# Two matmul passes for three in the values of a batch's last 64 tokens

## The chip, the cores and the metric

The kernel runs on one core of a Trainium2 chip. The metric is the device time of one execution in microseconds (us), and of several runs the median. Engines are named as in the profile: PE is TensorE's matmul, PEld its weight load, DVE is VectorE, ACT ScalarE, POOL GpSimd, SP SyncE, which here issues the DMAs.

## The reference, cut to what matters

Three layers follow each other on 8 batches of 576 tokens with 512 features: an attention over 32 memory slots, a token and channel mixing layer, and a last layer with four attention experts of head size 64. The change lies in the last layer:

```python
def _moe2_ref(x, w_gate, wq, wk, wv, wo):
    logits = x @ w_gate                    # 4 experts, the best 2 of a token count
    ...
    for e in range(E):                     # E = 4, Hd = 64
        q, k, v = x @ wq[e], x @ wk[e], x @ wv[e]
        scores = scale * (q @ k.transpose(0, 2, 1))
        ...                                # causal mask, softmax
        ye = a @ v @ wo[e]
        ...                                # ye is weighted by the gate of its token
```

The inputs are float32 and so is the result. A float32 matrix product is made here from three products of rounded parts: a matrix X is kept as a high part Xh (X rounded to the type fp32r that TensorE takes) and a low part Xl = X - Xh, and X W is taken as Xh Wh + Xh Wl + Xl Wh.

## The kernel before, in words

The kernel has three stages, one for each layer, in one program. In the last stage, which fills the time from about 694 us to the end, a batch's 576 tokens are five chunks of rows: four of 128 tokens and one of 64 (`rows`, `NQ = 5`, `ST = 64`, `SM = 512`). Tokens lie along the free axis of `xh[b]` and `xl[b]` (128 partitions x `KD = 4` pieces of the 512 features x 576 tokens).

`mm2_2(j, c)` makes piece c of half-batch j of this x (j = 2b and 2b + 1): a matmul into the PSUM ring `g`, an addition on DVE, the high part on ACT, the low part on POOL (L1233 to L1235). `load_2`, `load_p2`, `split_2` and `mm1_2` prepare the same layer of mixing for later half-batches; so the end of the second layer runs inside the last stage.

`values(b, c)` makes values and gate logits of chunk c: the chunk's tokens are the stationary operand (up to 128 columns), and the moving operand is `vgh` or `vgl`, high and low part of the 260 columns of `wv` (4 x 64) and `w_gate` (4). `mm3` (L250) issues 12 matmuls for it, three for each of the four feature pieces; with `late="l"` the four that use the low part of x come last. Then ACT copies the values' high part to the tiles `vhl` and `vh3` (shown as `vh`, L1280) and the logits to `lg` (L1281, for the last chunk once more into the lower half, L1283), and DVE writes the low part beside it (L1285). For the chunk of 64 tokens ACT copies the finished 64 rows to partitions 64 to 127 as well (L1287), since the weights of its tokens are used there for a second expert.

`gates(b, ...)` turns the logits of all five chunks into the gate (DVE, one exponential on ACT; L1297 to L1320), `norm(n)` multiplies the softmax of expert n with it (L1369 to L1371 on DVE, L1379 on POOL), `turn` and `tail_turn` transpose the result on PE (L1398 to L1418), and `weigh` multiplies by the values (L1443), adds the two halves of the PSUM tile through the scratch tile `yb` (a copy on ACT, L1445, an addition on DVE, L1446), and splits the sum (L1449, L1450 on POOL; L1461 and L1462 for the tokens of the last chunk). `project` multiplies by `wo` and sends the output. For the last batch the tiles of `project` are in a pool `late`, which takes memory that other tiles have left; the projections of three earlier batches (`HELD`) are kept for the last batch as work between (`fetch`, L1469, loads them again).

PSUM is shared out in rings: `g` has 3 buffers (`GB`), `s` and `t` have 2, `y` has 1. The order of the instructions in this stage isn't the order of the code: the program is built with a planner that simulates the engines with costs of its own and puts an instruction into its engine's queue when its operands would be there. So a matmul of one product may stand between those of another, as the rows below show. The order is fixed once the program is built; on the chip each engine's queue runs strictly in it. SP's queue is one too, with all DMA issues of this stage: loads (L875, L879), the swaps between `qa` and `qb` (L1264, L1265), the queries of the last tokens to `qz` (L1345), and outputs (L1498 to L1501).

Of the kernel before, what the change touches and what calls it, by code (L numbers as in the profile page):

```python
# [10 lines left out]
F32 = mybir.dt.float32  # L11
F32R = mybir.dt.float32r
BF16 = mybir.dt.bfloat16
I32 = mybir.dt.int32
U32 = mybir.dt.uint32
AF = mybir.ActivationFunctionType
# [11 lines left out]
def f(ap):  # L28
    return ap.bitcast(F32)
# [181 lines left out]
def fused_kernel(ctx: ExitStack, tc, q, k, v, phi, w_tok1, w_tok2, w_ch1, w_ch2,  # L211
                 w_gate, wq, wk, wv, wo, out):
    nc = tc.nc
    B, H, S, D = q.shape
# [4 lines left out]
    E = wq.shape[0]  # L219
    KD = DM // 128  # L220
# [3 lines left out]
    SM = 512  # L224
    ST = S - SM
    scale = 1.0 / float(D) ** 0.5

    PE, ACT, DVE, POOL, SP = nc.tensor, nc.scalar, nc.vector, nc.gpsimd, nc.sync
# [5 lines left out]
    consts = ctx.enter_context(tc.tile_pool(name="consts", bufs=1, reuse_waits="tile"))  # L234
    ident = consts.tile([128, 128], F32, name="ident")
    make_identity(nc, ident[:])
    consts.tile([128, 8], F32, name="edge")
    still = consts.tile([128, 128], BF16, name="still")
    DVE.memset(still[:], 0.0)

    def mm3(ps, pairs, start=True, stop=True, late=None):

# [74 lines left out]
    with ExitStack() as sa:  # L317
# [9 lines left out]
        t1l = wa.tile([128, 5, T], F32R, name="t1l")  # L327
        t2h = wa.tile([128, 2, S], F32R, name="t2h")
        t2l = wa.tile([128, 2, S], F32R, name="t2l")
        ones = wa.tile([128, 16], F32, name="ones")  # L330
        DVE.memset(ones[:], 1.0)
        vmask = wa.tile([128, 4, 64], F32, name="vmask")
# [569 lines left out]
    with ExitStack() as sb:  # L902
# [194 lines left out]
        for i in range(NW + LAG):  # L1097
            items = [()] if i == NW else [work[i]] if work[i][0] in WIDE else [(*work[i], 0), (*work[i], 1)]
            for it in items:
# [63 lines left out]
                if it and n == NBLK - 1 and fcs == [0]:  # L1163
                    sw_ctx.close()
                    wkx_ctx.close()
                    stg = stg_ctx.enter_context(tc.tile_pool(name="stgc", bufs=2, reuse_waits="tile"))
                    wcp = ctx.enter_context(tc.tile_pool(name="wcp", bufs=1, side="right"))
                    qkh = wcp.tile([128, 2, KD, E * 64], F32R, name="qkh")
                    qkl = wcp.tile([128, 2, KD, E * 64], F32R, name="qkl")
                    vgh = wcp.tile([128, KD, E * 64 + 16], F32R, name="vgh")[:, :, 0:E * 64 + E]  # L1170
                    vgl = wcp.tile([128, KD, E * 64 + 16], F32R, name="vgl")[:, :, 0:E * 64 + E]
                    woh = wcp.tile([128, 2, DM], F32R, name="woh")
                    wol = wcp.tile([128, 2, DM], F32R, name="wol")
                    w3 = w3_ctx.enter_context(tc.tile_pool(name="w3", bufs=1, side="right"))
                    wcl = chload()
# [10 lines left out]
    with ExitStack() as sc:  # L1186
# [10 lines left out]
        POOL.tensor_copy(tmask[ST:128, :], cmask[ST:128, SH + ST:S + ST])  # L1197
        qz = wk_.tile([128, 2, 2, 128], F32R, name="qz")
        POOL.memset(f(qz[:]), 0.0)
        tri = wk_.tile([128, E, E], F32, name="tri")  # L1200
        POOL.memset(tri[:], 1.0)
        POOL.affine_select(out=tri[:], in_=tri[:], compare_op=OP.is_gt, fill=0.0, base=0,
# [2 lines left out]
        NQ = 5  # L1205
# [17 lines left out]
        def mm2_2(j, c):  # L1223
            b = j // 2
            if j % 2 == 0 and c == 0:
                xh[b] = wk_.tile([128, KD, S], F32R, name="xh", bufs=1)
                xl[b] = wk_.tile([128, KD, S], F32R, name="xl", bufs=1)
            p = pp.tile([128, 512], F32, name="g", bufs=GB)[:, 0:SH]
            mm3(p, [((w2h[fc][:, c, :], w2l[fc][:, c, :]), (h2[j, fc][0][:], h2[j, fc][1][:]))
                    for fc in range(KM, KF)], late="r")  # L1230
            x_ = p2[j][:, c, :]
            ss = slice(SH * (j % 2), SH * (j % 2) + SH)
            DVE.tensor_add(x_, x_, p)  # L1233
            ACT.activation(xh[b][:, c, ss], x_, AF.Copy)  # L1234
            POOL.tensor_sub(xl[b][:, c, ss], x_, f(xh[b][:, c, ss]))  # L1235

        def proj(b, pr, i, hf, early=False):

# [28 lines left out]
        def values(b, c):  # L1267
            if c == 0:
                vhl[b] = ((late or wk_).tile([128, NQ, E - 1, 128], F32R, name="vhl", bufs=1),
                          (late or wk_).tile([128, NQ, 1, 128], F32R, name="vh3", bufs=1 if late else 2))  # L1270
            L = lgb[b % 2]
            r = rows[c]
            cs = slice(128 * c, 128 * c + r)
            p = pp.tile([128, 512], F32, name="g", bufs=GB)
            mm3(p[0:r, 0:E * 64 + E], [((xh[b][:, kd, cs], xl[b][:, kd, cs]), (vgh[:, kd, :], vgl[:, kd, :]))
                                       for kd in range(KD)], late="l")
            pv = p[0:r, 0:E * 64].rearrange("p (e h) -> p e h", e=E)
            parts = [(vhl[b][0], pv[:, 0:E - 1, :]), (vhl[b][1], pv[:, E - 1:E, :])]
            for t, x in parts:
                ACT.activation(t[0:r, c, :, 0:64], x, AF.Copy)  # L1280
            ACT.activation(L[0:r, c, :], p[0:r, E * 64:E * 64 + E], AF.Copy)  # L1281
            if c == NQ - 1:
                ACT.activation(L[r:128, c, :], p[0:r, E * 64:E * 64 + E], AF.Copy)  # L1283
            for t, x in parts:
                DVE.tensor_sub(t[0:r, c, :, 64:128], x, f(t[0:r, c, :, 0:64]))  # L1285
                if c == NQ - 1:
                    ACT.activation(t[r:128, c, :, :], f(t[0:r, c, :, :]), AF.Copy)  # L1287

# [183 lines left out]
        def project(b, c):  # L1472
            last = c == NQ - 1
            if last and b % 2 == 0:
                return
            cs = slice(0, 128) if last else slice(128 * c, 128 * c + 128)
            if b == B - 1 and c == 1:
                for i, w in enumerate((slice(0, 256), slice(256, 512))):
                    p = pp.tile([128, 512], F32, name="g", bufs=GB)[:, 0:256]
                    mm3(p, [((y[0][:, cs], y[1][:, cs]), (woh[:, pr, w], wol[:, pr, w]))  # L1480
                            for pr in range(2) for y in [yT[b, pr][1:]]], late="l")
                    o_ = late.tile([128, 256], F32, name=f"oh{i}")
                    if i:
                        DVE.tensor_copy(o_[:], p)
                    else:
                        ACT.activation(o_[:], p, AF.Copy)
                    SP.dma_start(out[b, cs, w], o_[:])
                return
            p = pp.tile([128, 512], F32, name="g", bufs=GB)
            mm3(p[:], [((y[0][:, cs], y[1][:, cs]), (woh[:, pr, :], wol[:, pr, :]))  # L1490
                       for pr in range(2) for y in [yE[b // 2, pr] if last else yT[b, pr][1:]]], late="l")
            o_ = late.tile([128, 512], F32, name="osb", bufs=2) if late else wk_.tile([128, 512], F32, name="osb", bufs=2)
            if b == B - 1 and c in (3, 0):
                DVE.tensor_copy(o_[:], p[:])
            else:
                ACT.activation(o_[:], p[:], AF.Copy)
            if last:
                SP.dma_start(out[b - 1, SM:S, :], o_[0:ST, :])  # L1498
                SP.dma_start(out[b, SM:S, :], o_[ST:128, :])
            else:  # L1500
                SP.dma_start(out[b, cs, :], o_[:])  # L1501
# [3 lines left out]
        late = None  # L1505
# [165 lines left out]
```

## Time and profile before

| | |
|---|---|
| median of 3 runs | 1177.72 us (1177.28 to 1179.32) |
| profiled execution, its own time | 1178.92 us |
| its span, first to last instruction | 1177.2 us |
| PE busy | 1154.5 us (98% of the span), 8658 matmuls |
| DVE, ACT, POOL busy | 783.8, 591.6, 407.4 us |
| granted TensorE clock | 0.999 of 2.4 GHz |

In a timeline each row is a run of like instructions of one engine: start in us from the span's start, duration in us, engine, line of the code, operation, tiles written and read, shapes, count, and in brackets the idle time before it and what ended that. A matmul's duration (0.28 us for 260 columns) is the time through the pipeline; the next one starts earlier, so what a matmul costs is read from the distance of starts. Weight loads (PEld) run beside matmuls.

### The profile page before, as it was taken

The page shows a single profiled execution, that of the slowest core. Times are in us where ns is not written, and L with a number is a line of the kernel's source. Part 1 is how long each engine was busy: PE and PEld are TensorE (multiplying, and loading weights), DVE is VectorE, ACT ScalarE, POOL GpSimd, SP SyncE. Part 2 cuts the span into 40 slices and gives each one's busy share as a digit, 9 for nine tenths or more (in the row PEclk, how much of TensorE's full clock was granted, in tenths as well). Part 3 has the DMA queues.
Part 4 walks back from the last instruction along what each step waited for, and adds up shares of the span by engine and source line. Part 5 has one row for each costly group of instructions (what it writes and reads, how often), then busy time and mean ns, then how long its engine had stood idle before and what let it go on. Part 6 is the DMA issues. An engine that isn't in the chain of part 4 may idle for free.

```text
span 1177.2 us, 23497 instructions
## 1 busy us (share of the span) xinstructions
PE 1154.5 (98%) x8658; PEld 1051.0 (89%) x8658; DVE 783.8 (67%) x1942; ACT 591.6 (50%) x1533; POOL 407.4 (35%) x575
## 2 busy tenths in 40 slices
PE   7899999999999999999999999999999999999998
PEld 6788888888899999999998889999999999999986
DVE  6889998485565665746553624876666777686763
ACT  3566775442322232322221214777676767676774
POOL 2867766000101010100100545647272737373331
PEclk9999999999999999999999999999999999999999
DMA  8989974451121221303020453323332333222423
GB/s 246 250 258 294 293 240 157 134 177 39 37 72 36 72 70 39 107 1 107 34 67 29 133 151 109 88 68 98 76 101 69 107 95 108 72 84 72 151 88 108
DMA packets 125843, 133.53 MB, mean 113 GB/s; under 512 B 36000, under 2 KB 95392, under 8 KB 125728
## 3 DMA queue, kind: packets, MB, share of 16 engines
q1 hardware_dynamic: 125728, 132.03, 37.5%
q8 instruction: 68, 1.11, 0.4%
q14 instruction: 47, 0.39, 0.1%
HBM read 89.01 MB, written 31.46 MB: 102 GB/s over the span
## 4 chain that ended last, share of the span: by engine, by line
PE 84%; DVE 7%; DMA 3%; POOL 2%; issue 2%; ACT 1%; SPq 1%; ACTq 0%; DVEq 0%; POOLq 0%
PE g L250 24%; PE o L250 21%; PE h L250 19%; PE y L1443 4%; PE s L1334 3%; PE t L1398 3%; PE s L1356 1%; DMA qn<-in_q_dram 1%; PE g L437 1%; POOL a L1379 1%; DMA cst<-in_moe_w_tok_dram 1%; PE g L676 1%; PE g L670 1%; PE t L250 1%; PE g L679 1%
## 5 line engine op out<-in xcount | busy, mean ns | idle before, releaser
L982 POOL TENSOR_TENSOR tl<-ub,th 128x512 fp32r<-128x512 f32 x12 | 18.5, 1561 | 362.3 <-DVE tl L982 362.3
L250 PE MATMUL o<-hl,w2h 128*128 128x512 f32 x360 | 141.0, 392 | 0.0
L250 PE MATMUL o<-hh,w2l 128*128 128x512 f32 x360 | 140.3, 390 | 0.0
L250 PE MATMUL o<-hh,w2h 128*128 128x512 f32 x360 | 134.9, 392 | 0.0
L1379 POOL TENSOR_TENSOR a<-a,cf 128x128 f32<-128x128 f32 (+3 forms) x128 | 88.1, 721 | 69.1 <-DVE cf L1371 65.2
L934 ACT ACTIVATE hh<-m 128x256 fp32r<-128x256 f32 x120 | 48.9, 417 | 125.0 <-DVE m L1005 65.9
L1323 DVE CUSTOM_DVE_ANT_0 ssb<-s,cmask 128x128 f32<-128x128 f32 (+2 forms) x144 | 68.5, 483 | 25.4 <-PE s L1334 17.4
L1336 ACT ACTIVATE a<-ssb,nb 128x128 f32<-128x128 f32 (+3 forms) x128 | 71.3, 558 | 19.0 <-DVE nb L1323 14.9
L250 PEld LDWEIGHTS o<-hh,w2l 128*128 128x128 f32 x360 | 67.6, 188 | 14.5
L250 PEld LDWEIGHTS o<-hh,w2h 128*128 128x128 f32 x360 | 67.6, 188 | 12.4
L250 PEld LDWEIGHTS o<-hl,w2h 128*128 128x128 f32 x360 | 67.9, 188 | 11.9
L250 PE MATMUL h<-uh,w1l 128*128 128x256 f32 (+2 forms) x232 | 76.6, 331 | 0.0
L250 PE MATMUL h<-uh,w1h 128*128 128x256 f32 (+2 forms) x232 | 76.2, 330 | 0.0
L250 PE MATMUL h<-ul,w1h 128*128 128x256 f32 (+2 forms) x232 | 76.1, 332 | 0.0
L935 DVE SCALAR_TENSOR_TENSOR hl<-m,hh 128x256 fp32r<-128x256 f32 x120 | 58.7, 498 | 17.9 <-ACT hh L934 15.2
L250 PE MATMUL g<-xh,qkh 128*128 128x288 f32 x232 | 65.5, 301 | 0.0
L1235 POOL TENSOR_TENSOR xl<-p,xh 128x288 fp32r<-128x288 f32 x60 | 47.4, 808 | 48.5 <-ACT xh L1234 48.4
L250 PE MATMUL g<-xh,qkl 128*128 128x288 f32 x232 | 64.0, 296 | 0.0
L998 ACT ACTIVATE m<-h 128x256 f32<-128x256 f32 x30 | 11.5, 385 | 101.3 <-PE h L250 101.3
L1000 DVE TENSOR_TENSOR m<-m,h 128x256 f32<-128x256 f32 x30 | 12.6, 421 | 70.7 <-PE h L250 70.1
L257 DVE TENSOR_TENSOR Bl<-t,Bh 128x512 fp32r<-128x512 f32 (+1 forms) x80 | 50.5, 633 | 13.4 <-ACT Bh L254 12.2
L254 ACT ACTIVATE Bh<-t 128x512 fp32r<-128x512 f32 (+1 forms) x80 | 43.9, 552 | 15.4 <-PE t L1398 6.4
(332 smaller groups left out, 3810.2 us busy)
## 6 DMA issues: line engine op xcount, KB each, us to landing
cst<-in_moe_w_ch_dram SPq DMA_DIRECT2D x24, 512.0 KB, 4.1
u_d<-u SPq DMA_DIRECT2D x32, 288.0 KB, 3.3
ub<-u_d SPq DMA_DIRECT2D x9, 1024.0 KB, 5.0
u<-u_d SPq DMA_DIRECT2D x16, 576.0 KB, 4.0
p<-x_d SPq DMA_DIRECT2D x15, 576.0 KB, 4.0
qn<-in_q_dram SPq DMA_DIRECT2D x16, 512.0 KB, 6.0
kv<-in_k_dram SPq DMA_DIRECT2D x16, 512.0 KB, 5.9
kv<-in_v_dram SPq DMA_DIRECT2D x16, 512.0 KB, 5.6
```

The lines of the kernel that those rows point to most:

```text
L250: PE.matmul(ps, lhsT=a, rhs=b, start=start and i == 0, stop=stop and i == len(seq) - 1)
L254: ACT.activation(hi, src, AF.Copy)
L257: DVE.tensor_sub(lo, src, f(hi))
L934: ACT.activation(hh, c, AF.Relu)
L935: DVE.scalar_tensor_tensor(hl, c, 0.0, f(hh), op0=OP.max, op1=OP.subtract)
L1235: POOL.tensor_sub(xl[b][:, c, ss], x_, f(xh[b][:, c, ss]))
L1323: DVE.tensor_tensor_reduce(out=out, in0=p, in1=mask, scale=-scale, scalar=least, op0=OP.add, op1=OP.min, accum_out=acc)
L1334: PE.matmul(p[:, 0:W], lhsT=q_[n][:, 128 * c:128 * c + 128], rhs=kk[n][:, 0:W], start=(i == 0), stop=(i == 1))
L1336: ACT.activation(a[:, aoff[c]:aoff[c] + W], s_[:, 0:W], AF.Exp, scale=-1.0, bias=nb[:, 0:1], accum_out=sm[:, c:c + 1])
L1379: POOL.tensor_mul(x_, x_, cf[:, c:c + 1].to_broadcast([128, W]))
L1398: PE.transpose(p[:, 128 * kc:128 * kc + 128], a[:, o + 128 * kc:o + 128 * kc + 128], ident[:])
L1443: PE.matmul(p[:, lo:w], lhsT=v_[:, kc, 0, :], rhs=x, start=(i == 0), stop=(i == len(ops) - 1))
```

## The change

For the chunk of 64 tokens alone, the high and the low part of x come side by side into a tile `xt` (128 x 4 x 128): two DMAs per batch from `xh` and `xl`, issued from SP after the last piece of x is made. One matmul with 128 stationary columns then gives Xh Wh in rows 0 to 63 of the PSUM tile and Xl Wh in rows 64 to 127; Xh Wl goes to rows 0 to 63 with 64 stationary columns as before. That is 8 matmuls for 12. The two halves are added in SBUF: ACT copies the lower half to a `yb` buffer, DVE adds the upper half. High part and logits are then taken from this SBUF tile by ACT, and the low part is made on POOL, where it was on DVE.

Memory for `xt` (2 KB in a partition) comes from three other edits: `still` (a zero tile for matmuls that fill PE's pauses in the first stage) goes from the pool that lives to the end into one of the first stage; `vgh` and `vgl` lose their padding from 272 to 260 columns; and the two output tiles `oh0` and `oh1` of the last batch are taken from the earlier `osb` buffers.

```diff
-    still = consts.tile([128, 128], BF16, name="still")
-    DVE.memset(still[:], 0.0)
...
+        still = wa.tile([128, 128], BF16, name="still")
+        DVE.memset(still[:], 0.0)
...
-                    vgh = wcp.tile([128, KD, E * 64 + 16], F32R, name="vgh")[:, :, 0:E * 64 + E]
-                    vgl = wcp.tile([128, KD, E * 64 + 16], F32R, name="vgl")[:, :, 0:E * 64 + E]
+                    vgh = wcp.tile([128, KD, E * 64 + E], F32R, name="vgh")
+                    vgl = wcp.tile([128, KD, E * 64 + E], F32R, name="vgl")
...
+        xt = wk_.tile([128, KD, 128], F32R, name="xt")
...                                             # in mm2_2, after the low part of a piece
+            if j % 2 and c == KD - 1:
+                for i, x in enumerate((xh, xl)):
+                    SP.dma_start(f(xt[:, :, ST * i:ST * i + ST]), f(x[b][:, :, SM:S]))
...                                             # in values
-            mm3(p[0:r, 0:E * 64 + E], [((xh[b][:, kd, cs], xl[b][:, kd, cs]), (vgh[:, kd, :], vgl[:, kd, :]))
-                                       for kd in range(KD)], late="l")
+            W = E * 64 + E
+            if c < NQ - 1:
+                mm3(p[0:r, 0:W], [((xh[b][:, kd, cs], xl[b][:, kd, cs]), (vgh[:, kd, :], vgl[:, kd, :]))
+                                  for kd in range(KD)], late="l")
+            else:
+                for kd in range(KD):
+                    PE.matmul(p[:, 0:W], lhsT=xt[:, kd, :], rhs=vgh[:, kd, :], start=kd == 0, stop=kd == KD - 1)
+                    if kd < KD - 1:
+                        for k in (kd,) if kd else (KD - 1, 0):
+                            PE.matmul(p[0:r, 0:W], lhsT=xt[:, k, 0:r], rhs=vgl[:, k, :], start=False, stop=False)
+                x_ = wk_.tile([128, 320], F32, name="yb", bufs=2)[:, 0:W]
+                ACT.activation(x_[0:r, :], p[r:128, 0:W], AF.Copy)
+                DVE.tensor_add(x_[0:r, :], p[0:r, 0:W], x_[0:r, :])
+                p = x_
...
-                DVE.tensor_sub(t[0:r, c, :, 64:128], x, f(t[0:r, c, :, 0:64]))
+                (DVE if c < NQ - 1 else POOL).tensor_sub(t[0:r, c, :, 64:128], x, f(t[0:r, c, :, 0:64]))
...                                             # in project, the two halves of one chunk of the last batch
-                    o_ = late.tile([128, 256], F32, name=f"oh{i}")
+                    o_ = wk_.tile([128, 512], F32, name="osb", bufs=2)[:, 0:256]
```

## Rows read from the trace of the kernel before

**Rows 1.** The page: busy time of each engine, chain by engine

```profile
PE 1154.5 (98%) x8658; PEld 1051.0 (89%) x8658; DVE 783.8 (67%) x1942; ACT 591.6 (50%) x1533; POOL 407.4 (35%) x575
...
PE 84%; DVE 7%; DMA 3%; POOL 2%; issue 2%; ACT 1%; SPq 1%; ACTq 0%; DVEq 0%; POOLq 0%
```

**Rows 2.** Busy time by stretch (start:end, length, then PE, PEld, DVE, ACT, POOL)

```profile
720.00:780.00 60.00, 59.58 (x458) 58.68 (x457) 44.48 (x144) 42.30 (x132) 32.66 (x51) 1.00 0.37 102
...
1020.00:1080.00 60.00, 58.96 (x444) 57.26 (x443) 45.21 (x150) 43.92 (x126) 32.93 (x51) 1.00 0.27 74
...
1130.00:1177.00 47.00, 41.05 (x237) 34.84 (x235) 22.24 (x63) 28.61 (x70) 11.19 (x17) 0.99 0.35 117
```

**Rows 3.** Waits of PE from 690 us on: total, times, longest (first and last)

```profile
PE g L250 <- ACT osb L1496: 1.3, 3, 0.7
...
PE g L250 <- DVE qb L1259: 0.2, 1, 0.2
```

**Rows 4.** Timeline of PE, chunk of 128 tokens (last batch), first matmul and the next product

```profile
1116.59 0.28 PE L250 MATMUL g<-vgh,xh 128*128 128x260 f32 x1
...
1118.04 0.69 PE L1356 MATMUL s<-kk,qz 128*128 128x288 f32 x4
```

**Rows 5.** Timeline of PE, chunk of 64 tokens (first batch), and the next product

```profile
730.48 0.28 PE L250 MATMUL g<-vgh,xh 128*64 128x260 f32 x1
...
731.91 0.30 PE L250 MATMUL g<-xh,qkh 128*128 128x288 f32 x1
...
732.04 0.29 PE L250 MATMUL g<-xh,qkl 128*128 128x288 f32 x1
```

**Rows 6.** One tile's instructions: weight loads beside vgl (ns shortest/median/longest)

```profile
L250 PEld LDWEIGHTS g<-vgl,xh x160: 133/188/192, 719.1 to 1121.2; 128*128 128x128 f32 x128, 128*64 128x64 f32 x32
```

**Rows 7.** Groups by line and shape from 700 us on (busy us, mean ns)

```profile
L1445 ACT ACTIVATE yb<-y 64x256 f32<-64x256 f32 x32 | 12.2, 381 | 3.6 <-PE y L1443 2.9
...
L1446 DVE TENSOR_TENSOR yt<-y,yb 64x256 f32<-64x256 f32 x32 | 13.3, 415 | 4.3 <-ACT yb L1445 2.4 <-POOL yel L1462 1.3
...
L1285 DVE TENSOR_TENSOR vhl<-g,vhl 64x192 fp32r<-64x192 f32 x8 | 2.8, 349 | 5.2 <-ACT lg L1283 5.1
...
L1285 DVE TENSOR_TENSOR vh<-g,vh 64x64 fp32r<-64x64 f32 x8 | 1.6, 205 | 0.0
...
L1450 POOL TENSOR_TENSOR yl<-yt,yh 128x256 fp32r<-128x256 f32 x30 | 22.1, 736 | 84.3 <-ACT yh L1449 74.2 <-ACT lg L1281 7.1 <-issue 2.9
...
L1462 POOL TENSOR_TENSOR yel<-yt,yeh 128x64 fp32r<-128x64 f32 x16 | 5.2, 328 | 9.7 <-ACT yeh L1461 9.7
```

**Rows 8.** Timeline of the second batch: ACT's copy, POOL's work, DVE's gate, PE's transposes

```profile
786.10 0.52 ACT L1287 ACTIVATE vhl<-vhl 64x384 fp32r<-64x384 f32 x1 [0.42 <-DVE vhl L1285]
...
788.72 0.74 POOL L1450 TENSOR_TENSOR yl<-yt,yh 128x256 fp32r<-128x256 f32 x1 [4.30 <-ACT yh L1449]
...
790.92 2.75 POOL L1379 TENSOR_TENSOR a<-a,cf 128x128 f32<-128x128 f32 x4 [1.17 <-DVE cf L1371]
...
789.98 0.17 DVE L1320 COPY gate<-gate 64x2 f32<-64x2 f32 x1
...
794.66 0.81 PE L1398 MATMUL t<-ident,a 128*128 128x128 f32 x6
```

**Rows 9.** One tile's instructions: DVE's last step of norm (ns shortest/median/longest)

```profile
L1371 DVE TENSOR_TENSOR cf<-cf,gate x32: 145/166/847, 742.7 to 1151.9; 128x5 f32<-128x5 f32 x16, 128x4 f32<-128x4 f32 x16
```

**Rows 10.** DMA issues from 700 us on (KB each, median us to landing)

```profile
u<-u_d SPq DMA_DIRECT2D x14, 576.0 KB, 4.0
```

**Rows 11.** Timeline: last pieces of xl on POOL, SP's next issues, first use

```profile
1090.72 3.10 POOL L1235 TENSOR_TENSOR xl<-p,xh 128x288 fp32r<-128x288 f32 x4 [5.30 <-ACT xh L1234]
...
1093.85 0.33 SPq L1469 DMA_DIRECT2D yh<-y_d  x1
...
1103.89 0.48 PE L250 MATMUL g<-woh,yh 128*128 128x512 f32 x1
...
1120.46 0.28 PE L250 MATMUL g<-vgh,xh 128*64 128x260 f32 x1
```

More of the change, by code (lines that the diff above doesn't have):

```diff
@@ L1481, in project @@
                             for pr in range(2) for y in [yT[b, pr][1:]]], late="l")
-                    o_ = late.tile([128, 256], F32, name=f"oh{i}")
+                    o_ = wk_.tile([128, 512], F32, name="osb", bufs=2)[:, 0:256]
                     if i:
-                        DVE.tensor_copy(o_[:], p)
+                        DVE.tensor_copy(o_, p)
                     else:
-                        ACT.activation(o_[:], p, AF.Copy)
-                    SP.dma_start(out[b, cs, w], o_[:])
+                        ACT.activation(o_, p, AF.Copy)
+                    SP.dma_start(out[b, cs, w], o_)
                 return
```

## The prediction

> **What bounds the kernel now.** I read the page first: PE is busy for 1154.5 of 1177.2 us, and 84% of the chain that ended last is PE [rows 1]. A busy PE need not be a full one, so the second view is busy time by stretch, for the last stage alone, where the change lies. There PE is busy for 59.58 us of 60 in the first stretch and 58.96 in the least full of six up to 1080 us, at full clock, while DVE, ACT and POOL have 44 to 45, 42 to 44 and 33 [rows 2]. Third, PE's waits from 690 us on: nine kinds, from 1.3 us down to 0.2, together 5.6 us in 487 us [rows 3]. Only the last 47 us, with 41.05 busy, are looser, and even there the longest wait of PE is short; much of the rest is the last output on its way. So the stage is bound by the number of matmuls and what each costs. A matmul taken away is worth its distance to the next start; work added on another engine costs only where PE then runs out of things that are ready.
>
> **The change part by part.**
>
> *Matmuls taken away.* A chunk of 128 tokens takes twelve matmuls from 1116.59 to 1118.04, 0.121 us each [rows 4]; the chunk of 64 takes twelve from 730.48 to 731.91, 0.119 us each [rows 5]. The step follows the 260 moving columns, not the width of the stationary operand. Eight batches lose four each: 32 x 0.1193 = 3.82 us. Four of the remaining eight get 128 stationary columns for 64. Their load lasts 188 instead of 133 ns [rows 6], but the step with the wide load is 0.121 against 0.119, so it stays beside the matmuls: 32 x 0.002 = 0.06 us. If that cover were gone it would cost 32 x 0.055 = 1.8 us. I take -3.8.
>
> *The padding of vgh and vgl.* A row now starts every 1040 bytes for 1088, which is no multiple of 64. None of the rows read has such an operand. From below nothing; from above I take the nearest larger matmul, 288 columns, which takes 0.13 us from start to start [rows 5] where 260 take 0.119: 0.011 us on each of the 42 matmuls a batch that don't start at piece 0 (3 of 4 pieces in 4 x 12 + 8), 336 in all, 3.7 us. I take nothing, since all columns still lie next to each other.
>
> *The way out of PSUM.* Added per batch: an ACT copy of 64 x 260 (0.38 us by the 64 x 256 copy of weigh) and a DVE addition (0.42 by its partner); taken from DVE are 0.35 and 0.21 us [rows 7]. ACT gains 3.1 us of work in all, DVE loses 1.1, on engines with a quarter of their time free [rows 2]. The logits come 0.8 us later plus two handovers, for which I take 0.15 us each: 1.1, less the 0.48 by which the matmuls end sooner, so the gate starts 0.6 us later. What hides that: PE's other ready work. In the second batch the gate is done at 790.15, POOL multiplies from 790.92, and the first transposes start at 794.66 [rows 8], while PE had no gap. Cover gone, it costs 0.6 x 8 = 4.8 us. The PSUM buffer itself is free sooner (after one copy and one addition instead of four copies and two subtractions), which can only help.
>
> *The low part on POOL.* Two subtractions of 64 x 192 and 64 x 64. Between 328 ns for 64 columns and 736 for 256 [rows 7], 192 columns come to 0.60 by a straight line: 0.93 us per batch. ACT's copy to the lower half (L1287) waits for the first; before, it waited 0.42 us for DVE [rows 8]. ACT's queue is strict, so what stands behind that copy waits too: eviction of `g` and `t`, exponentials. POOL had been idle for 4.30 us before 788.72 [rows 8], so the wait is 0.6 plus at worst the 1.06 us of L1450 and L1462 [rows 7], less than PE's cover: with one `g` buffer stuck there are two more, each twelve matmuls of 0.13 us [rows 5], 3.1 us. I take nothing.
>
> DVE and POOL also get in each other's way. Norm's last step on DVE takes 166 ns by the median and 847 at the longest [rows 9]. The Trainium skill (SBUF — State Buffer, "SBUF: two separate sides") has a rule for this: a POOL operation and a DVE operation with two SBUF inputs exclude each other for a whole instruction. By it the gate's first steps, which read SBUF twice and come just then, could stand behind both subtractions; the sum by it would change only in the gate's lateness, which is the first rival.
>
> *The two DMAs.* 16 issues on SP, some 0.5 us each, wait for the last subtraction of xl. In the last batch that ends at 1093.82, and the tile is read at 1120.46: 26 us, for 2 x 128 KB, where 576 KB landed 4.0 us after the issue [rows 10, 11]. Queued behind are the loads L1469 at 1093.85 and, in other batches, the loads for half-batches to come (L875). They slip by 1.1 us; the first use of L1469's tiles is at 1103.89, ten us after the issue [rows 11]. I take nothing.
>
> *Memory.* `still`, `osb` and the shifted addresses change which old tile a new one must wait for. A gain or loss of some tenths at the borders of stages can't be excluded; I take nothing.
>
> *The order.* The planner lays out the whole stage anew. PE's 5.6 us of waits are the bound on both sides: all gone, or twice as many. They are few already, and four matmuls per batch that could fill a pause are missing, so I take a loss, 0.6 us.
>
> Sum: -3.8 + 0.6 = -3.2 us. The profiled execution took 1178.92 us (span 1177.2 and 1.7 around it), 1.2 above the median of the runs shown. 1178.92 - 3.2 = 1175.7; by the median 1177.72 - 3.2 = **1174.5 us**. All times below are by the median.
>
> **The rivals.** (1) *The gate comes late and PE runs dry.* To the 0.6 us come up to 0.93 of DVE behind POOL, 1.5 us. For it: gate, norm, multiplication and transpose are a chain. Against it: 3.7 us lie between multiplication and transpose in the second batch, of which the multiplication of the first three blocks needs no more than the 2.75 of all four [rows 8]. If half the batches lose half of it, 4 x 0.75 = 3.0: -3.8 + 3.0, 1176.9 us, no measurable change.
>
> (2) *Slower: ACT parks behind POOL at L1287.* If the planner puts that copy behind a POOL run that lasts longer than it thinks, 2.75 us of multiplication, 1.06 of L1450 and L1462 and 0.93 of the subtractions [rows 7, 8] hold ACT for 4.7 us; beyond 3.1 PE stops, 1.6 us in eight places, 13 us: 1187 us. It decides from 3.6 us on (3.1 + 0.48 saved). Against it: those multiplications need this batch's gate and so come later, as in the second batch.
>
> (3) *The matmuls that stay get dearer*, by the weight loads (1.8 us) or the rows off 64 bytes (up to 3.7): 1174 to 1178, around 1176.5. Against it: the step with wide loads. The Trainium skill (SBUF — State Buffer, "Door 1: The DMA port swizzle") speaks of lines of 16 bytes; 1040 is a multiple of that, so by it the padding costs nothing, and the sum is as above; no run here shows it.
>
> **How the numbers follow.** The forecast has 0.59, rival 1 (and other stalls of the new order) 0.24, rival 2 0.08, rival 3 0.09. The likeliest case itself spans -5 to -2.4: 1172.7 to 1175.3. The range 1172.6 to 1178.4 takes in rivals 1 and 3 and leaves out a still better order (0.06) and the slower cases. Of this kernel 0.2% is about what can be told from no change: 2.36 us, 1175.4 to 1180.1. Faster gets 0.59; no change rivals 1 and 3 less what of them ends slower, 0.31; slower rival 2 and that rest, 0.10.
>
> **What would show it.** Right: 8626 matmuls for 8658, the last chunk's eight some 0.12 us apart, PE's waits from 690 us on between 4 and 8 us. Rival 1: waits of the transposes L1398 or of `weigh` on POOL or ACT. Rival 2: ACT's wait before L1287 on POOL well over 1 us, and PE's waits for ACT. Rival 3: steps over 0.125 us for 260 columns. I am wrong if PE's waits grow by more than 1.4 us, or if matmuls were not what ended last.

## The result and the profile after

The changed kernel takes 1187.84 us (median of 6 runs, 1186.34 to 1189.26) against 1179.05 of the kernel before in the same comparison (6 runs, 1177.28 to 1181.01): ratio 1.0071 [1.0061, 1.0081]. By the ratio it is 8.4 us slower, by the medians 8.8. Forecast was a gain of 3.2 us. The execution that was profiled took 1186.34 us.

The page of the changed kernel, answering to [rows 1]: 32 matmuls fewer, and PE is busy longer. So the lost time isn't added work of PE; where it went, busy time alone doesn't say.

```profile
PE 1157.5 (98%) x8626; PEld 1049.6 (89%) x8626; DVE 783.7 (66%) x1934; ACT 595.8 (50%) x1541; POOL 415.0 (35%) x591
...
PE 79%; DVE 10%; DMA 4%; ACT 3%; POOL 1%; issue 1%; SPq 1%; ACTq 0%; DVEq 0%; POOLq 0%
```

The timeline of PE in a chunk of 64 tokens (third batch), answering to [rows 5]. From 843.99 to 844.82 are seven steps, 0.119 us each, as before: the matmuls that stay are no dearer.

```profile
843.99 0.28 PE L1285 MATMUL g<-vgh,xt 128*128 128x260 f32 x1
844.10 0.40 PE L1288 MATMUL g<-vgl,xt 128*64 128x260 f32 x2
...
844.82 0.28 PE L1285 MATMUL g<-vgh,xt 128*128 128x260 f32 x1
```

PE's waits from 690 us on (engine, what waits, for whom: us in total, times, longest; the first four), answering to [rows 3]: eleven kinds with 12.3 us for nine with 5.6. No row names `xt` or a DMA: PE never waits for the two added transfers. The row for POOL is new; it is a single wait of 2.0 us.

```profile
PE g L248 <- DVE p L1234: 3.2, 4, 1.8
PE g L248 <- ACT osb L1512: 2.6, 5, 0.8
PE t L1414 <- POOL a L1395: 2.0, 1, 2.0
PE t L1414 <- DVE Bl L255: 1.1, 1, 1.1
```

Where does it begin? The timeline of the second batch, answering to [rows 8]. The last matmul of the chunk starts at 784.68, as early as before (784.69).

```profile
787.23 0.43 ACT L1461 ACTIVATE yb<-y 64x320 f32<-64x320 f32 x1 [0.70 <-PE y L1459]
787.57 0.37 ACT L1290 ACTIVATE yb<-g 64x260 f32<-64x260 f32 x1
...
788.83 0.74 POOL L1466 TENSOR_TENSOR yl<-yt,yh 128x256 fp32r<-128x256 f32 x1 [3.58 <-ACT yh L1465]
...
789.41 0.20 ACT L1299 ACTIVATE lg<-yb 64x4 f32<-64x4 f32 x1
789.53 0.32 POOL L1478 TENSOR_TENSOR yel<-yt,yeh 128x64 fp32r<-128x64 f32 x1
...
789.81 0.59 POOL L1301 TENSOR_TENSOR vhl<-yb,vhl 64x192 fp32r<-64x192 f32 x1
...
791.34 0.52 ACT L1303 ACTIVATE vhl<-vhl 64x384 fp32r<-64x384 f32 x1
...
794.80 0.17 DVE L1336 COPY gate<-gate 64x2 f32<-64x2 f32 x1
795.24 5.48 POOL L1395 TENSOR_TENSOR a<-a,cf 128x128 f32<-128x128 f32 x8 [4.56 <-DVE cf L1387]
...
801.26 0.82 PE L1414 MATMUL t<-ident,a 128*128 128x128 f32 x6
```

The values' copy out of PSUM (L1290) comes at 787.57, 2.9 us after the last matmul, right behind the copy of `weigh` (L1461), which itself had waited 0.70 us for PE. Both take their buffer from the ring `yb`, and a ring is given out in the order in which it is planned. Before, the values needed no buffer of it, and `weigh`'s copy came behind the values (ACT in the same batch of the kernel before):

```profile
785.52 0.17 ACT L1283 ACTIVATE lg<-g 64x4 f32<-64x4 f32 x1
...
786.84 0.43 ACT L1445 ACTIVATE yb<-y 64x320 f32<-64x320 f32 x1
```

So the logits are complete at 789.61 for 785.69, the gate at 794.97 for 790.15, and the first transposes start at 801.26 for 794.66 [rows 8]. POOL's subtractions stand behind two of `weigh`'s (788.83, 789.53), and ACT's copy to the lower half moves from 786.10 to 791.34.

Before, six transposes at 794.66 were what PE did while ACT and DVE emptied the `g` buffers. In the changed kernel PE goes on to scores and products of the mixing layer, uses up the ring `g`, and stops (same batch, PE's timeline):

```profile
797.00 0.30 PE L248 MATMUL g<-hh,w2h 128*128 128x288 f32 x1
...
798.38 0.40 PE L1350 MATMUL s<-kk,qb 128*128 128x512 f32 x1
799.56 0.40 PE L248 MATMUL g<-hh,w2h 128*128 128x288 f32 x1 [0.79 <-ACT osb L1512]
```

ACT's copy that PE waits for here had itself waited 2.87 us until an earlier output had left its buffer `osb`. SP issued that output only at 795.41, behind four of the swaps between `qa` and `qb` (791.23 to 794.83); in the kernel before, the first output stands behind three and goes at 792.73. So the lost time reaches PE by way of ACT's and SP's queues, and PE's own row names only the last link (same batch, SP and ACT):

```profile
794.83 0.54 SPq L1268 DMA_DIRECT2D qa<-qb  x1
795.41 1.86 SPq L1517 DMA_DIRECT2D out_dram<-osb  x2
798.91 1.23 ACT L1512 ACTIVATE osb<-g 128x512 f32<-128x512 f32 x2 [2.87 <-DMA out_dram<-osb]
```

The last batch is worst. Its copy stands behind three of `weigh`'s and comes 7.7 us after the last matmul (1123.38). PE has nothing left after 1138.51 and waits for the multiplication on POOL (timeline, ACT, POOL and PE):

```profile
1123.31 0.43 ACT L1461 ACTIVATE yb<-y 64x320 f32<-64x320 f32 x1 [0.65 <-PE y L1459]
...
1126.80 0.38 ACT L1461 ACTIVATE yb<-y 64x256 f32<-64x256 f32 x1
...
1130.74 0.43 ACT L1461 ACTIVATE yb<-y 64x320 f32<-64x320 f32 x1
1131.08 0.37 ACT L1290 ACTIVATE yb<-g 64x260 f32<-64x260 f32 x1
...
1137.43 5.47 POOL L1395 TENSOR_TENSOR a<-a,cf 128x128 f32<-128x128 f32 x8 [3.35 <-DVE cf L1387]
...
1138.51 0.39 PE L1350 MATMUL s<-kk,qb 128*128 128x512 f32 x1
1140.95 0.88 PE L1414 MATMUL t<-ident,a 128*128 128x128 f32 x6 [2.05 <-POOL a L1395]
```

### The profile page after: what moved, and what is told of

Its sections match the earlier page's. It is cut to its first block, busy times and chain, and to the rows that moved or that the text cites. A ratio compares the mean times of both kernels' runs of the same rounds, so it can differ in the third digit from the quotient of the medians.

```text
span 1184.6 us, 23440 instructions
## 1 busy us (share of the span) xinstructions
PE 1157.5 (98%) x8626; PEld 1049.6 (89%) x8626; DVE 783.7 (66%) x1934; ACT 595.8 (50%) x1541; POOL 415.0 (35%) x591
## 4 chain that ended last, share of the span: by engine, by line
PE 79%; DVE 10%; DMA 4%; ACT 3%; POOL 1%; issue 1%; SPq 1%; ACTq 0%; DVEq 0%; POOLq 0%
PE g L248 21%; PE o L248 21%; PE h L248 19%; PE y L1459 4%; PE t L1414 2%; PE s L1350 2%; PE s L1372 1%; DMA qn<-in_q_dram 1%; ACT a L1352 1%; DMA cst<-in_moe_w_tok_dram 1%; PE t L248 1%; PE g L676 1%; DMA p<-x_d 1%; PE g L670 1%; DVE ssb L1339 1%
## 5 line engine op out<-in xcount | busy, mean ns | idle before, releaser
L1395 POOL TENSOR_TENSOR a<-a,cf 128x384 f32<-128x384 f32 (+3 forms) x128 | 88.1, 722 | 52.6 <-DVE cf L1387 46.9
L1352 ACT ACTIVATE a<-ssb,nb 128x128 f32<-128x128 f32 (+3 forms) x128 | 71.4, 559 | 17.9 <-DVE nb L1339 10.9
L1236 POOL TENSOR_TENSOR xl<-p,xh 128x288 fp32r<-128x288 f32 x60 | 47.7, 811 | 38.8 <-ACT xh L1235 38.8
```

What stands on the lines that cost most here:

```text
L1352: ACT.activation(a[:, aoff[c]:aoff[c] + W], s_[:, 0:W], AF.Exp, scale=-1.0, bias=nb[:, 0:1], accum_out=sm[:, c:c + 1])
L1395: POOL.tensor_mul(x_, x_, cf[:, c:c + 1].to_broadcast([128, W]))
```

## The experiments

The theories, by the letters that the expectations use: (A) the gate comes late and PE runs dry, in the first runs through the ring `yb` above all; (B) the work added on ACT and POOL costs by itself; (C) memory or dearer matmuls; (D) the planner's new order costs, whatever made it new. Sixteen kernels were run, each against the kernel before on the same chip (medians of that 1179.4 to 1179.8 us). mm_only and mm_pad leave the product Xl Wh of the last chunk out of the result, cut and drop Xh Wl; add4 adds Xl Wl.

Two numbers are read from every trace. *Gate end*: from the start of the chunk's last matmul to the end of the gate's last copy (L1320, now L1336), mean of the eight batches. *Stage*: from the start of the first values matmul behind PE's wait of 0.42 us near 724 us to the start of the kernel's last matmul. The stage leaves out the first stages, whose end differs by a microsecond from run to run.

| kernel | matmuls per chunk | gate end | stage | ratio, interval |
|---|---|---|---|---|
| before | 12 | 7.36 | 448.2 | 1 |
| changed | 8 | 10.83 | 456.1 | 1.0071 [1.0061, 1.0081] |
| mem_moves | 12 | 7.35 | 448.9 | 0.9998 [0.9990, 1.0006] |
| tie_only | 12 | 9.16 | 453.3 | 1.0038 [1.0024, 1.0052] |
| own_scratch | 8 | 9.31 | 453.3 | 1.0056 [1.0038, 1.0073] |
| own_dve | 8 | 9.37 | 451.1 | 1.0022 [1.0014, 1.0031] |
| dve_ring | 8 | 10.93 | 460.8 | 1.0099 [1.0083, 1.0114] |
| mm_only | 8 | 7.55 | 448.5 | 0.9991 [0.9982, 1.0000] |
| gate_first | 8 | 7.76 | 448.7 | 1.0004 [0.9995, 1.0012] |
| gate_delay | 12 | 9.28 | 452.8 | 1.0032 [1.0020, 1.0045] |
| cut | 8 | 7.41 | 445.0 | 0.9966 [0.9954, 0.9979] |
| drop | 8 | 7.52 | 447.9 | 0.9987 [0.9978, 0.9996] |
| add4 | 16 | 7.39 | 451.5 | 1.0028 [1.0016, 1.0039] |
| replan | 12 | 7.48 | 449.1 | 1.0005 [0.9996, 1.0014] |
| mm_pad | 8 | 7.63 | 446.0 | 0.9976 [0.9967, 0.9985] |
| gate_pad | 8 | 7.44 | 448.5 | 0.9993 [0.9984, 1.0001] |
| own_pad | 8 | 9.26 | 455.7 | 1.0065 [1.0048, 1.0082] |
| after_pad | 8 | 10.31 | 456.2 | 1.0062 [1.0050, 1.0074] |

### Memory, the ring, and POOL

**mem_moves**: the kernel before with the three memory edits alone (`still`, `vgh` and `vgl` without padding, `oh0` and `oh1` from `osb`; the first two groups of the diff above).

> The three memory edits alone (zero tile in the first stage's pool, 260 columns for 272, the last outputs in the ring osb), values as before with twelve matmuls, no xt. Theories A and B: ratio 0.998 to 1.002 (1177 to 1181 us). Theory C: most of the loss is here, 1.004 to 1.009; with dear rows the step of 260 columns is over 0.125 us for 0.120.

0.9998: nothing that can be told, and theory C is out.

**tie_only**: the kernel before, where only the last chunk's way out goes through the ring.

```diff
+            if c == NQ - 1:
+                x_ = wk_.tile([128, 320], F32, name="yb", bufs=2)[:, 0:E * 64 + E]
+                ACT.activation(x_[0:r, :], p[0:r, 0:E * 64 + E], AF.Copy)
+                p = x_
```

> The kernel before, with one part of the change alone: the last chunk's PSUM tile (twelve matmuls, no halves) is copied by ACT to a buffer of the ring yb, and high part, logits and low part are taken from there. Theory A: slower than before without any other edit, 1182 to 1190 us (ratio 1.003 to 1.010), with copies several us after the last matmul in some batches. Theories B and C: 1.000 to 1.002, eight copies of 0.38 us on ACT beside other work.

One copy of 0.38 us through the ring costs 4.5 us, as theory A said. The gate is 1.8 us later in the mean. In the second and the last batch the copy waits for the ring and comes 2.8 and 3.8 us after the last matmul, and there the gate is 5.7 and 5.6 us later; in the other six the copy comes after 0.4 to 0.5 us, and the gate is 0.5 us later in the mean.

**own_scratch**: the changed kernel with a buffer of its own for the sum. The memory for it comes from `yeh` and `yel` with 3 buffers for 4, which leaves all queues in the order that they have without it.

```diff
-                x_ = wk_.tile([128, 320], F32, name="yb", bufs=2)[:, 0:W]
+                x_ = wk_.tile([128, W], F32, name="xs")
```

> The change, with a scratch tile of its own for the sum of the two halves instead of a buffer of the ring yb (room for it: yeh and yel get 3 buffers for 4). Theory A (the ring yb ties the way out of PSUM to weigh: in the changed kernel the copy L1290 ran 2.7, 2.7, 3.5 and 7.4 us after the last matmul in four of eight batches, each time only after weigh's copies; gate and PSUM buffer are late): the copy comes within 1 us in most batches, PE's waits from 700 us on fall from 12 us towards 6, and the time is at or below the kernel before, 1174 to 1179 us (ratio 0.996 to 1.000). Theory B (POOL's two subtractions and ACT waiting for them): no change, 1186 to 1189 (1.006 to 1.009). Theory C (memory moves and rows off 64 bytes): no change either. Theory D (any new order of the planner costs that much): 1180 to 1190, without a pattern.

**own_dve** is the same with the two subtractions on DVE, **dve_ring** has them on DVE and keeps the ring.

```diff
-                (DVE if c < NQ - 1 else POOL).tensor_sub(t[0:r, c, :, 64:128], x, f(t[0:r, c, :, 0:64]))
+                DVE.tensor_sub(t[0:r, c, :, 64:128], x, f(t[0:r, c, :, 0:64]))
```

> As own_scratch, and the two subtractions of the last chunk on DVE again. Theory A: within 2 us of own_scratch (ratio 0.996 to 1.001). Theory B: 3 us or more faster than own_scratch. C: as the changed kernel.

> The changed kernel with one edit: the two subtractions on DVE in place of POOL; the scratch buffer still comes from the ring that the weighing uses. If ring and POOL add up: own_dve lay 4.1 us below own_scratch, so 1187.8 - 4 = 1184, ratio 1.0035. If the ring is what makes the subtractions late (they sit behind the ring's copies on POOL only because the copy comes late), POOL is worth little here: 1187, ratio 1.006. If POOL is all of it: 1182.6, ratio 1.002 as own_dve.

In own_scratch the copy runs 0.3 to 0.4 us after the last matmul in every batch, the gate is 1.5 us earlier than in the changed kernel, and the stage 2.8 us shorter. But theory A had the whole loss gone, and 6.6 of the 8.4 us remain: the ring alone is not the cause. With the subtractions on DVE another 4 us go by the ratios (2.1 by the stage), as theory B said, though the gate is no earlier. Then dve_ring went the other way, which none of its expectations had. Its busy time of PE by stretch shows why it can't be set beside the others (start:end, length, PE busy, granted clock, DMA share, GB/s):

```profile
1090.00:1092.00 2.00, 1.77 (x12) 0.91 0.00 0
1092.00:1094.00 2.00, 2.00 (x10) 0.50 0.00 0
1094.00:1096.00 2.00, 2.00 (x14) 0.74 0.28 66
...
1142.00:1144.00 2.00, 0.78 (x4) 0.71 0.27 65
1144.00:1146.00 2.00, 1.63 (x8) 0.50 0.34 131
1146.00:1148.00 2.00, 2.00 (x11) 0.50 0.00 0
1148.00:1150.00 2.00, 2.00 (x12) 0.59 0.00 0
```

After two waits of PE of 1.97 us each the granted clock falls to 0.50, the lower of the two levels (1.2 GHz). The share missing from full clock, summed over these rows, is 1.7 + 3.4 = 5.1 us, an estimate of what it can cost at most, and about the 4.7 by which its stage is longer than that of the changed kernel. So what POOL's part costs is not settled.

### The gate alone

**mm_only**: stacked operand, DMAs and eight matmuls as in the changed kernel, but the halves are not added, and the chunk leaves PSUM as before.

```diff
-                x_ = wk_.tile([128, 320], F32, name="yb", bufs=2)[:, 0:W]
-                ACT.activation(x_[0:r, :], p[r:128, 0:W], AF.Copy)
-                DVE.tensor_add(x_[0:r, :], p[0:r, 0:W], x_[0:r, :])
-                p = x_
```

> The changed kernel's eight matmuls, stacked operand and its DMAs, but the two halves of PSUM are not added: the chunk is evicted straight from the upper 64 partitions, as before, with the subtractions on DVE. The product of the tokens' low part with the weights' high part is left out. Theory A (the changed kernel loses by the longer way from the last matmul to the gate): the matmuls' saving comes through, 32 x 0.119 = 3.8 us, 1176.0 for 1179.8, ratio 0.9968, and the gate ends 7.3 to 7.5 us after the last matmul as in the kernel before. Theory D (any new order of the last stage, or the DMAs, cost the time): 1181 to 1184, ratio 1.001 to 1.004.

The 8.4 us are gone, so they came with the way out of PSUM: the sum, its buffer and POOL's part. But of the saving only 1.1 us is left, between both expectations; the runs on the matmuls and the order below take this up.

**gate_first**: own_dve, with the four logit columns added first and straight into `lg`.

```diff
+                g_ = slice(E * 64, W)
+                ACT.activation(x_[0:r, g_], p[r:128, g_], AF.Copy)
+                DVE.tensor_add(L[0:r, c, :], p[0:r, g_], x_[0:r, g_])
+                DVE.tensor_add(L[r:128, c, :], p[0:r, g_], x_[0:r, g_])
...                                             # then columns 0 to 255 as in own_dve
```

> As own_dve, but the four logit columns leave PSUM first (one ACT copy of 64 x 4 and two DVE additions straight into the logits), and the 256 value columns behind them. Theory A (lateness of the gate is what costs): the gate ends 8 us after the last matmul or sooner (9.4 in own_dve, 7.4 before), and the time is 1176 to 1178.5, ratio 0.997 to 0.999. Theory B (the work added to ACT and DVE costs, whatever comes first): 1182 to 1184, ratio 1.002 to 1.004, since this has one ACT instruction and two DVE instructions more and two ACT copies less than own_dve.

The gate is 1.6 us earlier than in own_dve, the time 2.1 us less, with more work on DVE. It moves as the theory of the late gate says; the level, 1.0004, lies between both expectations.

**gate_delay**: the reverse, in the kernel before. Only the four logit columns make a detour.

```diff
+            l_ = p[0:r, E * 64:E * 64 + E]
+            if c == NQ - 1:
+                for i in range(2):
+                    l1, l2 = (wk_.tile([128, E], F32, name=f"l{i}{k}")[0:r, :] for k in range(2))
+                    ACT.activation(l1, l_, AF.Copy)
+                    DVE.tensor_copy(l2, l1)
+                    l_ = l2
...                                             # both copies to lg read l_
```

> The kernel before, with twelve matmuls, where only the four logit columns of the last chunk go through two more pairs of copies (ACT, DVE, ACT, DVE; 64 x 4 each) before they reach the logits. Nothing else is added. Theory A (lateness of the gate alone costs): the gate ends some 2 us later, 9.4 us after the last matmul, and the time rises by 3 to 6 us, ratio 1.0025 to 1.005. Theory B (the values' way, the scratch buffer and POOL cost, not the gate's lateness): 1179.8 to 1180.8, ratio 1.000 to 1.001.

The gate ends 1.9 us later (second batch, timeline of ACT, DVE and POOL, beside 789.98 and 790.92 in [rows 8]), and the time rises by 3.8 us. Nothing but these small copies is added, but the stage is planned anew, so what its order is worth is in the 3.8.

```profile
786.70 0.21 ACT L1288 ACTIVATE lg<-l 64x4 f32<-64x4 f32 x1
...
793.55 0.16 DVE L1327 COPY gate<-gate 64x2 f32<-64x2 f32 x1
794.00 5.47 POOL L1386 TENSOR_TENSOR a<-a,cf 128x128 f32<-128x128 f32 x8 [4.29 <-DVE cf L1378]
```

That is 2.0 us of time for each us of lateness over the eight batches, with an order's worth in it (another order of the kernel before, replan below, differs by 0.6 us). What speaks for the gate against the order is the whole table. Set to twelve matmuls per chunk, at 3.8 us for four, the stage is 447.7 to 452.5 us in the ten kernels with a gate at 7.4 to 7.8 us, 452.8 to 459.5 in the five with 9.2 to 9.4, and 459.9 to 464.6 in the three with 10.3 to 10.9. The groups don't overlap, though nearly every kernel has an order of its own. So a late gate costs; how much for each us isn't sharp, since within a group the stage varies by 5 to 7 us.

### The matmuls alone, and the order

**cut**: the kernel before as planned; after planning the 32 matmuls Xh Wl of the last chunks are taken out of PE's queue. All other entries of all queues stay in their order.

```diff
+    cut = {i.name for bb in blocks for i in bb.instructions if ...}    # vgl with 64 columns of xh
+    for bb in blocks:
+        bb.instructions = [i for i in bb.instructions if i.name not in cut]
```

> The kernel before with every queue in exactly its order, only the 32 matmuls high part of the tokens x low part of the weights of the last chunks are taken out (four a batch; that product is left out of the result). Theory P (in a fixed order a matmul is worth its step on PE, 0.119 us, and the saving was eaten by the new order and the late gate): 3.5 to 3.8 us less, 1176.0 to 1176.3 for 1179.8, ratio 0.9968 to 0.9971. Theory W (PE's pace is set by other engines as well, so that the saved steps turn into waits of PE): 0.5 to 1.5 us less, ratio 0.9988 to 0.9996.

**drop** leaves the same matmuls out in the code, so the stage is planned anew. **add4** has four more (Xl Wl, ahead of Xl Wh). **replan** is add4 as planned, with these 32 taken out afterwards: the instructions of the kernel before in another order.

```diff
+                seq = [(xh, vgh, kd) for kd in range(KD)] + [(xl, vgh, kd) for kd in range(KD)]       # drop
```

> The same 32 matmuls left out, but in the code, so that the planner lays out the stage anew. With theory P and an order as good as the old one: ratio 0.997, as cut. If the planner's new order costs what it seemed to cost where only the matmuls were changed (4 us of new waits for 3.8 us of steps, ratio 0.9991): 1178 to 1180, ratio 0.9985 to 1.000. With theory W also 0.999, and then cut shows the same.

> The kernel before with four matmuls more per batch in the last chunk (low part of the tokens x low part of the weights), planned anew. Theory P: +3.8 us and the new order's own, 1183 to 1185, ratio 1.0025 to 1.0045. Theory W: the added steps fill waits, 1180 to 1181, ratio 1.0005 to 1.001.

> The order that was planned for add4, from which the 32 added matmuls are then taken out: exactly the instructions of the kernel before in another planned order. It measures what another order is worth by itself. Theory P: 3.8 us below add4. If orders differ by little: 0.9995 to 1.0005 against before; if a new order costs by itself some 2 to 4 us: 1.002 to 1.0035.

In a fixed order the matmuls are worth 4.0 us (1.5 around it; 3.2 by the stage), 0.125 each: theory P. add4 agrees from the other side, with 3.3 us for 32 more. PE's waits stay what they were, here the first two of nine rows of cut:

```profile
PE g L250 <- DVE p L1233: 1.4, 2, 1.0
PE g L250 <- ACT osb L1496: 1.3, 3, 0.7
```

Planned anew (drop), 1.5 us are left. New waits stand in the way, above all for transfers whose data PE did not wait for before (two of nine rows):

```profile
PE s L1340 <- DMA qa<-qb: 0.8, 2, 0.6
PE s L1362 <- DMA qz<-qb: 0.7, 1, 0.7
```

So the planner's order for eight matmuls gives back 2.5 us (2.9 by the stage). It isn't that any new order does: replan has another one and stays at 1.0005.

### Both together

Four kernels of those above in the order that the planner makes with four more matmuls in the chunk (Xl Wl from `xt`), which are taken out afterwards as in replan: **mm_pad** from mm_only, **gate_pad** from gate_first, **own_pad** from own_dve, **after_pad** from the changed kernel.

```diff
+                            PE.matmul(p[0:r, 0:W], lhsT=xt[:, k, r:128], rhs=vgl[:, k, :], start=False, stop=False)
                             PE.matmul(p[0:r, 0:W], lhsT=xt[:, k, 0:r], rhs=vgl[:, k, :], start=False, stop=False)
```

> As mm_only (eight stacked matmuls, halves not added, the product of the tokens' low part with the weights' high part left out of the result), in the order planned for twelve matmuls. If the planner's order for eight was what ate the saving: 1176, ratio 0.9965 to 0.9975, near cut. If the stacked matmuls or the two DMAs cost something by themselves: 0.999 as mm_only.

> As gate_first (whole computation; logits out first, own buffer, subtractions on DVE), in the order planned for twelve matmuls. If order and late gate are the whole loss: 1176 to 1178, ratio 0.997 to 0.9985, faster than the kernel before. If the sum in SBUF has a price of its own beside the gate: 1.000 as gate_first.

> As own_dve (whole computation; own buffer, subtractions on DVE, logits behind the 256 value columns), in the order planned for twelve matmuls. The gate some 2 us late as in gate_delay (+3.8) and the saving of cut (-4.0): 1179.6, ratio 0.9990 to 1.0010. If planning for eight was not what cost: 1.002 as own_dve.

> The changed kernel as it is, in the order planned for twelve matmuls. If the late gate (3.5 us later through ring and POOL) costs about 2 us for each us, some 7 us, less the saving of 4: 1182 to 1184, ratio 1.002 to 1.0035. If the order for eight is most of the loss: 1180, ratio 1.000. If the planning made no difference here: 1187.8, ratio 1.007.

mm_pad comes close to cut, 2.8 us below the kernel before: between the two lie 1.2 us for stacked operand, wide loads, DMAs and another order together, and where the gate is early the order for eight was most of what ate the saving. gate_pad, the whole computation, comes to 0.9993, between its expectations. It lies 2 us above mm_pad with the gate as early, so the sum in SBUF or its order costs that, and no single wait of PE shows where (eleven kinds, the longest 0.7). It beats the changed kernel by 0.8% and can't be told from the kernel before; no version here that computes the whole result beats that.

own_pad missed by far. It has own_dve's instructions and its gate end (9.26 and 9.37), and takes 5 us more: with a late gate, orders of the same work differ by as much as the effect. Some of this is the clock: in its profiled execution the granted clock falls to 0.50 once (rows at the end), which can be 1.7 us of it. after_pad stays at 1.0062, where planning was to make no difference, so for the changed kernel the order for eight was not the matter. Beside own_pad its gate is 1 us later for no more time: here 2.0 us for each us does not hold.

## Why the prediction was wrong

- *Matmuls taken away, -3.8 us*: right as the worth of 32 steps in a fixed order (cut, -4.0; -3.2 by the stage). The wide loads stayed covered (step 0.119).
- *Padding and memory, nothing*: right (mem_moves, 0.9998). The Trainium skill (SBUF — State Buffer, "Door 1: The DMA port swizzle") speaks of lines of 16 bytes, and the trace agrees, with no price for rows every 1040 bytes.
- *DMAs, nothing*: right; PE never waits for `xt`.
- *The way out of PSUM: the gate 0.6 us later, hidden by PE's other ready work.* This is the step that failed, twice. The size: 1.1 us behind the last matmul is what the gate's first step lost where nothing stood ahead (own_scratch, 2.52 us after the last matmul for 1.45). But I took the copy for one that can run at once. Its buffer comes from a ring that `weigh` uses, which the prediction doesn't mention, and in four of eight batches it stood behind `weigh`'s copies: the gate's first step came 5.0, 5.2, 6.4 and 10.1 us after the last matmul. And along the gate's own chain the lateness grew: in own_scratch the exponential is 1.8 us late and the gate's end 2.0, since its steps stand between others on ACT and DVE and meet POOL's work (in the first batch the gate's last copy takes 0.70 us for 0.17, beside a subtraction for `xl`, L1236). The cover: I read it from a PE without gaps. gate_delay shows that it is not whole: 1.9 us of lateness cost 3.8. By that the bound for lost cover, 8 us for each us of lateness in eight batches, was four times too high; the value taken, nothing, was the wrong end. And PE's waits, which were not to grow by more than 1.4 us, grew by 6.7.
- *Low part on POOL, nothing*: open in its size. ACT's copy to the lower half did come late, by 3.8 us against the kernel before (5.33 for 1.51 us behind the last matmul, mean). But ACT didn't wait there: it is idle for 0.03 us at most before that copy (L1303) in all eight batches. With a buffer of its own the copy comes at 2.99 us (own_scratch), and with the subtractions on DVE at 2.91 (own_dve); so 2.3 us of the lateness are the ring's and 0.1 POOL's. The exclusion of DVE and POOL is there: the gate's first step on DVE beside POOL's subtractions, and in own_dve without them (ns shortest/median/longest), then the first two steps in the second batch:

```profile
L1313 DVE TENSOR_TENSOR g<-lg x8: 279/339/439, 733.8 to 1133.5; 128x80 f32<-128x80 f32 x8
```

```profile
L1313 DVE TENSOR_TENSOR g<-lg x8: 227/238/243, 734.6 to 1127.0; 128x80 f32<-128x80 f32 x8
```

```profile
789.64 0.30 DVE L1313 TENSOR_TENSOR g<-lg 128x80 f32<-128x80 f32 x1 [0.17 <-ACT lg L1299]
789.87 0.63 DVE L1314 TENSOR_TENSOR g<-lg 128x80 f32<-128x80 f32 x1
```

  Both steps read SBUF twice. POOL's subtractions at 789.53 and 789.81 (above) end at 789.85 and 790.40, the two steps 0.10 us after them. The same 0.10 us holds for all 27 of these steps in the changed kernel and own_scratch that begin beside one of POOL's subtractions. By the rule of the Trainium skill (SBUF — State Buffer, "SBUF: two separate sides") one of the two engines stands behind the other's whole instruction. The trace agrees: the step waits for the end of the subtraction that is running. Since that is often nearly over, the two steps lose 0.2 us a batch, and with POOL the gate is no later than with DVE (9.31 and 9.37). What POOL's part costs beside the gate is open.
- *The order, +0.6 us*: mis-sized. With the same early gate it is +2.5 (drop against cut), within the bounds that I gave.
- *Rivals.* The first, the gate late and PE dry, had the mechanism, with 1176.9 us: I gave it 1.5 us of lateness, and half of that in half the batches. Measured are 3.5 us in the mean, from 1.3 in the third batch to 7.8 in the last, and its sign came, transposes that wait for POOL (L1414, 2.0 us). The second had the time (1187) by luck: ACT didn't wait at L1287, now L1303; own_dve, without POOL, still loses 2.6 us, and tie_only, with its subtractions on DVE, 4.5.

What the runs give: -4.0 for the matmuls and +2.5 for the order make -1.5, and mm_only has -1.1. From there to the changed kernel are 9.4 us. By the 2.0 us for each us of gate_delay, the gate's 3.3 us more (10.83 for 7.55) make some 6.5, an estimate that own_pad and after_pad do not bear out. The other 3 us are open: the sum's own work, POOL's part, and the order, which own_pad shows to be worth as much.

## What to carry to other kernels

A scratch tile from a ring that another stage uses puts the new work behind that stage's uses of it: read who takes the buffers before costing the copy. PE that never idles doesn't show that a later input is hidden; what PE does meanwhile was planned around the time at which that input came, so delay one input by a known amount, as in gate_delay, to get the price, and run a second order of the same work beside it to see how sharp that price is. Where a planner orders the work, take instructions out behind it once (as in cut) to separate their worth from the new order.

## What was not expected of the hardware

A wait of PE of about two microseconds can be followed by the lower clock or not. In dve_ring the granted clock fell to 0.50 after waits of 1.97 us, twice, while the changed kernel, after waits of 1.82 and 2.05 us near the same places, kept 1.00 (rows of its stretches):

```profile
1090.00:1092.00 2.00, 2.00 (x17) 1.00 0.00 0
...
1142.00:1144.00 2.00, 1.59 (x13) 1.00 0.25 93
1144.00:1146.00 2.00, 1.90 (x14) 1.00 0.00 0
```

own_pad has both in one execution: after a wait of 1.65 us that ends at 1038.64 the clock fell, after one of 2.17 us that ends at 1141.84 it stayed at 1.00.

```profile
1036.00:1038.00 2.00, 0.99 (x8) 1.00 0.11 34
1038.00:1040.00 2.00, 1.36 (x6) 0.70 0.00 0
1040.00:1042.00 2.00, 2.00 (x10) 0.50 0.00 0
1042.00:1044.00 2.00, 2.00 (x16) 0.94 0.00 0
```

So the length of the wait alone doesn't decide. No run tells what made the difference.
